# Chunks of 504, 504, 288, 504, 504 tokens in place of 512, 512, 256, 512, 512, and another order of steps around the third chunk

## The chip, the cores and the metric

The kernel runs on one core of a Trainium2 chip. The core has TensorE (PE, matrix products into PSUM), VectorE (DVE), ScalarE (ACT), GpSimd (POOL) and SyncE (SP, which issues most DMAs). The metric is the device time of one execution in microseconds (us), as the median of three runs.

## What is computed

Attention, then two feed-forward blocks, all in float32 on 4 x 576 = 2304 tokens of width 512 (d is 64 wide, 8 heads, scores under a mask of 32 keys: plain for heads 0 to 3, every fourth key for heads 4 to 7):

```python
attn = softmax(where(masks, q @ k.T / 8, -1e9)); x = attn @ v   # 2304 x 512
h = x @ w_in                       # 512 -> 2048
x = (h * (1 / (1 + exp(-h)))) @ w_out   # 2048 -> 512
h = ((x @ w1) * (x @ w2)) @ w3     # 512 -> 1024 -> 1024
out = h @ w_out2                   # 1024 -> 512
```

## The kernel before

Matrices are kept as two parts, a high one (float32 rounded to TensorE's fp32r format) and a low one (what is left), and a product is made of three matmuls: high by high, low by high, high by low.

**Stages.** The instructions of each engine stand in the order in which the program emits them. A list written out by hand (`START`) covers the attention of the first of the four batches, the first chunk of the first feed-forward block and the loading and splitting of `w_in` and `w_out`. Then come the other chunks with the attention of the other batches between them, then the second feed-forward block (lines 840 to 950: products of 384 columns, whose results are combined on VectorE).

**Chunks.** The first feed-forward block takes the tokens in five chunks (`CH1`: start and length). For each chunk it goes through 16 tiles f of 128 hidden units. For a tile, `h_part` makes 12 matmuls `h<-xT,wf` (line 707) with as many columns as the chunk has tokens. `g_tanh` takes half the argument's tanh on ACT (line 721), `g_mul` multiplies on DVE (line 725), `g_high` writes the high part on ACT (line 730) and `g_low` the low part on DVE (line 735). Then `x2_part` makes 12 matmuls `x<-g,wf` (line 747) of the same width into four PSUM banks, which add up over the 16 tiles. Each chunk thus has 16 x 24 = 384 such matmuls. At its end `x2_store` copies the four banks out on ACT and DVE and sends them to DRAM by two DMAs of SP.

**Ring.** The attention writes its output, transposed, into `xT`, which holds only `RING` tokens at a time: token a stands at place a modulo `RING`. `a_high` cuts a piece that goes over the ring's end into two. The fourth and fifth chunk stand where the first and second stood.

**Attention.** It runs in pairs of units (a unit is 192 queries of two heads). `ATT` gives the eight steps of a pair, and `att.step()` emits the next of them: V2S0 (the products with v of an earlier pair and the scores of this one, PE), M (maximum, DVE), E1O3 and E0O2 (exponentials of one unit, three on ACT, line 261, and the write of an earlier unit's output into `xT`, on ACT, line 330, and on DVE, line 323), N (sums and reciprocals on DVE, lines 269 and 271, then the scaling of both units on POOL, line 276), L (loads), T (transposes, PE, line 287) and W (their copy out of PSUM, ACT, line 298).

**Slots.** From the second chunk on, each tile has a slot, a string of letters that are emitted in that order. In the slot of tile f, `h` and `H` are the two halves of the h product of tile f+1, `t` its tanh and multiplication, `g` its high and low part, `x` and `X` the halves of the x product of tile f, `a` one attention step and `m` a piece of weight preparation. The third chunk's slot is the second entry of `SLOT` (index c - 1). Since eight attention steps make a pair and this slot has three, the steps that its three letters `a` stand for change from slot to slot.

```python
T2 = 384
NF = DFF // P      # 16 tiles
ATT = "V2S0|M0|E1O3|E0O2|N0|L1|T0|W0"
hps[c, f] = ps_h.tile([P, 512], F32, tag="h", name=f"h_{c}_{f}")
```

Of the kernel before, what the change touches and what calls it, by code (L numbers as in the profile page):

```python
# [31 lines left out]
KT = DM // P  # L32
NF = DFF // P
NG = DF2 // P
RING = 1280
CH1 = [(0, 512), (512, 512), (1024, 256), (1280, 512), (1792, 512)]
T2 = 384
NPR = NT // (2 * T2)
NSET = NG
# [31 lines left out]
ATT = "V2S0|M0|E1O3|E0O2|N0|L1|T0|W0"  # L71
SLOT = (
    ("ahaHaxtagX", "ahaHxataXg"),
    ("hHataxXag",) * 2,
    ("ahHaaaxtagaXaaa",) * 2,
    ("hmHmxtgmmmmXmmmm",) * 2,
)
# [12 lines left out]
def tile_kernel(  # L90
# [36 lines left out]
    stage = [base.tile([P, 2048], F32, tag=f"wf{NF // 2 + i}", name=f"stage{i}") for i in range(2 * NPAIR)]  # L127
    xT = base.tile([P, KT, 2, RING], F32R, tag="xT", name="xT")
    ident = base.tile([P, P], F32, tag="ident", name="ident")
# [195 lines left out]
    def a_high(n):  # L325
# [7 lines left out]
        def place(a, n_):  # L333

            first = min(n_, RING - a % RING)
            return [(0, first, a % RING)] + ([(first, n_ - first, 0)] if first < n_ else [])

# [7 lines left out]
        while r < DIL:  # L345
            cut = place(b * S + CL * r + mm * u, mm)
            x, n_ = cut[0][2], DIL - r
            while x + (n_ - 1) * CL + mm > RING:
                n_ -= 1
# [345 lines left out]

    NC1 = len(CH1)
    hps, gt, xps = {}, {}, {}
# [4 lines left out]
    def h_kt(c, f, kt):  # L702
        t0, n = CH1[c]
        ps = hps[c, f][:, :n]
        r0 = t0 % RING
        for x, (sa, sb) in enumerate(((0, 0), (1, 0), (0, 1))):
            nc.tensor.matmul(  # L707
                ps, win(f, sa, kt), xT[:, kt, sb, r0:r0 + n],
                start=(kt == 0 and x == 0), stop=(kt == KT - 1 and x == 2),
            )  # L710
# [7 lines left out]
    def g_tanh(c, f):  # L718
        n = CH1[c][1]
        gt[c, f] = gp.tile([P, 512], F32, tag="t", name=f"t_{c}_{f}", bufs=1)[:, :n]  # L720
        nc.scalar.activation(gt[c, f], hps[c, f][:, :n], AF.Tanh, scale=0.5)  # L721

    def g_mul(c, f):
        t, ps = gt[c, f], hps.pop((c, f))[:, :CH1[c][1]]
        nc.vector.scalar_tensor_tensor(t, t, 1.0, ps, op0=ALU.add, op1=ALU.mult)  # L725

    def g_high(c, f):
        n = CH1[c][1]
        g = gp.tile([P, 2, 512], F32R, tag="g", name=f"g_{c}_{f}")[:, :, :n]
        nc.scalar.activation(g[:, 0], gt[c, f], AF.Copy)  # L730
        gt[c, f] = g, gt[c, f]
# [6 lines left out]
    def x2_part(c, f, half):  # L738
        n = CH1[c][1]
        if f == 0 and half == 0:  # L740
            xps[c] = [ps_x.tile([P, 512], F32, tag="x", name=f"x2_{c}_{m}") for m in range(KT)]
        g = gt[c, f] if half == 0 else gt.pop((c, f))
        if half == 0 and type(g) is tuple:
            g = g[0]
        todo = [(m, sa, 0) for m in range(KT) for sa in (0, 1)] + [(m, 0, 1) for m in range(KT)]
        for m, sa, sb in todo[6 * half:6 * half + 6]:
            nc.tensor.matmul(  # L747
                xps[c][m][:, :n], wout(f, sa, m), g[:, sb],
                start=(f == 0 and sa == 0 and sb == 0), stop=(f == NF - 1 and sb == 1),
            )  # L750
# [26 lines left out]
    def b_part(name, hl):  # L777

        i = B_AT[name]
        if i < 2:  # L780
            o = (4 * i + 2 * hl) * RING
            return xflat[:, o:o + 2 * RING].rearrange("p (m t) -> p m t", m=2)[:, :, :T2]
# [402 lines left out]
```

## Time and profile before

| | |
|---|---|
| median of three runs | 809.15 us (809.12 to 811.04) |
| the profiled execution's own time | 809.15 us |
| its span, first to last instruction | 807.4 us |
| PE busy | 795.9 us (99%) |
| DVE busy | 478.2 us (59%) |
| ACT busy | 324.7 us (40%) |
| POOL busy | 55.8 us (7%) |
| mean granted TensorE clock | 0.997 |

The span is what the trace shows; 1.75 us of the time lie around it. The busy time of an engine counts each instruction from its start to its end, and PE's instructions overlap, so gaps between matmuls can hide in it. The spacing of their starts tells more. The granted clock is given as a share of 2.4 GHz.

### The profile page before, as it was taken

What the parts mean: (1) busy time and instruction counts of PE and PEld (TensorE: products, weight loads), DVE (VectorE), ACT (ScalarE), POOL (GpSimd) and SP (SyncE); (2) the same over time, 40 slices, a digit from 0 to 9 for tenths busy, and PEclk for the clock granted to TensorE, in tenths of its full rate; (3) what the DMA queues carried; (4) which work ended last, traced back from release to release, by engine and by line L of the source; (5) the groups of instructions that cost most, each with busy time, mean ns of one, the idle gap of its engine ahead of it and who ended that gap; (6) DMA issues with size and microseconds to landing.
All of it is one profiled execution on the core that took longest, in us unless ns stands there. A gap on an engine that the chain in (4) does not pass through costs nothing.

```text
span 807.4 us, 12941 instructions
## 1 busy us (share of the span) xinstructions
PE 795.9 (99%) x4882; PEld 689.6 (85%) x4882; DVE 478.2 (59%) x1175; ACT 324.7 (40%) x824; POOL 55.8 (7%) x90
## 2 busy tenths in 40 slices
PE   8899999999999999999999999999999999999997
PEld 7788888888889898888888887898889999999996
DVE  6889893533334342222478849588887655774444
ACT  7778773544434542222355536342333111321112
POOL 5010100010101100000000000013200000000000
PEclk9999999999999999999999999999999999999999
DMA  9967650403013002000387426328521660045202
GB/s 251 277 194 234 192 175 16 141 15 90 16 45 111 17 1 79 1 1 0 102 317 273 157 89 215 120 72 312 236 91 41 221 240 22 1 147 205 92 1 78
DMA packets 43454, 98.61 MB, mean 122 GB/s; under 512 B 3968, under 2 KB 21888, under 8 KB 41344
## 3 DMA queue, kind: packets, MB, share of 16 engines
q1 hardware_dynamic: 42784, 96.91, 36.6%
q10 hardware_dynamic: 608, 0.89, 0.4%
q8 instruction: 38, 0.62, 0.3%
q14 instruction: 24, 0.20, 0.1%
HBM read 73.66 MB, written 24.12 MB: 121 GB/s over the span
## 4 chain that ended last, share of the span: by engine, by line
PE 90%; DVE 3%; ACT 2%; DMA 1%; issue 1%; POOL 1%; SPq 0%; POOLq 0%; DVEq 0%; ACTq 0%
PE x L747 24%; PE h L707 24%; PE bank L867 20%; PE o L918 10%; PE wp L686 4%; PE o L231 2%; PE o L311 2%; PE t L287 2%; DMA raw_u<-in_w_out_dram 1%; ACT stage L261 1%; PE s L231 1%; DMA out_dram<-os 0%; ACT sm L261 0%; DVE y L559 0%; DVE wf L602 0%
## 5 line engine op out<-in xcount | busy, mean ns | idle before, releaser
L747 PE MATMUL x<-g,wf 128*128 128x512 f32 (+1 forms) x960 | 215.0, 372 | 2.7 <-ACT g L730 2.7
L707 PE MATMUL h<-xT,wf 128*128 128x512 f32 (+1 forms) x960 | 212.2, 370 | 0.0
L747 PEld LDWEIGHTS x<-g,wf 128*128 128x128 f32 x960 | 168.2, 190 | 33.6 <-ACT g L730 3.1
L707 PEld LDWEIGHTS h<-xT,wf 128*128 128x128 f32 x960 | 167.1, 188 | 30.5
L867 PE MATMUL bank<-xT,wf 128*128 128x384 f32 x864 | 164.5, 336 | 0.4
L867 PEld LDWEIGHTS bank<-xT,wf 128*128 128x128 f32 x864 | 151.4, 188 | 8.7 <-ACT s L885 1.1
L725 DVE SCALAR_TENSOR_TENSOR t<-t,h 128x512 f32<-128x512 f32 (+1 forms) x80 | 50.7, 633 | 123.4 <-ACT t L721 123.4
L918 PE MATMUL o<-wf,wf 128*128 128x512 f32 x432 | 110.7, 393 | 0.0
L721 ACT ACTIVATE t<-h 128x512 f32<-128x512 f32 (+1 forms) x80 | 44.2, 553 | 137.2 <-PE h L707 134.5
L918 PEld LDWEIGHTS o<-wf,wf 128*128 128x128 f32 x432 | 80.1, 188 | 12.8
L735 DVE TENSOR_TENSOR g<-t,g 128x512 fp32r<-128x512 f32 (+1 forms) x80 | 52.7, 659 | 42.6 <-ACT g L730 41.3
L730 ACT ACTIVATE g<-t 128x512 fp32r<-128x512 f32 (+1 forms) x80 | 47.0, 587 | 40.4 <-DVE t L725 40.4
L903 ACT ACTIVATE wf<-c 128x384 fp32r<-128x384 f32 x48 | 25.2, 525 | 86.8 <-DVE c L901 86.5
L885 ACT ACTIVATE s<-bank 128x384 f32<-128x384 f32 x24 | 11.7, 489 | 95.3 <-PE bank L867 84.7
L261 ACT ACTIVATE sm<-sm,nm 128x96 f32<-128x96 f32 x108 | 39.1, 365 | 22.6 <-DVE nm L251 22.6
L686 PE MATMUL wp<-wf,wf 128*128 128x512 f32 x192 | 46.8, 392 | 0.3 <-DVE wf L602 0.3
L276 POOL TENSOR_TENSOR sm<-sm,rs 128x288 f32<-128x288 f32 x36 | 27.5, 777 | 237.5 <-DVE su L269 126.8
L686 PEld LDWEIGHTS wp<-wf,wf 128*128 128x128 f32 x192 | 35.7, 188 | 7.4 <-DVE wf L602 0.7
L892 DVE TENSOR_TENSOR c<-u,bank 128x384 f32<-128x384 f32 x36 | 19.9, 553 | 32.0 <-PE bank L867 31.7
L598 ACT ACTIVATE wf<-y 128x512 fp32r<-128x512 f32 (+1 forms) x40 | 22.7, 584 | 28.5 <-DVE y L559 13.5
L251 DVE CUSTOM_DVE_ANT_0 sm<-o,mask 128x96 f32<-128x96 f32 x102 | 19.7, 254 | 17.5 <-PE o L231 17.3
L867 PE MATMUL bank<-wf,wf 128*128 128x384 f32 x144 | 28.9, 335 | 0.0
(96 smaller groups left out, 767.5 us busy)
## 6 DMA issues: line engine op xcount, KB each, us to landing
rawj<-in_w_dram SPq DMA_DIRECT2D x32, 512.0 KB, 3.7
raw_i<-in_w_in_dram SPq DMA_DIRECT2D x16, 512.0 KB, 4.3
raw_u<-in_w_out_dram SPq DMA_DIRECT2D x16, 512.0 KB, 4.6
setd<-wf SPq DMA_DIRECT2D x8, 1024.0 KB, 3.9
wf<-setd SPq DMA_DIRECT2D x8, 1024.0 KB, 5.2
setd<-wf SPq DMA_DIRECT2D x8, 768.0 KB, 5.9
wf<-setd SPq DMA_DIRECT2D x8, 768.0 KB, 7.3
xb<-x2d SPq DMA_DIRECT2D x12, 384.0 KB, 7.4
```

The costliest lines, as they stand in the source:

```text
L261: nc.scalar.activation(sm[:, j], sm[:, j], AF.Exp, bias=nm[:, j:j + 1], scale=-1.0, accum_out=su[:, j:j + 1],)
L276: nc.gpsimd.tensor_tensor(sm, sm, rs[:, :NB].to_broadcast([P, NB, KB]), op=ALU.mult)
L686: nc.tensor.matmul(wp_ps[i], a[:, i // 2, sa, i % 2 * P:(i % 2 + 1) * P], o[:, sb], start=(jt == 0 and x == 0), stop=(jt == NG - 1 and x = ...
L707: nc.tensor.matmul(ps, win(f, sa, kt), xT[:, kt, sb, r0:r0 + n], start=(kt == 0 and x == 0), stop=(kt == KT - 1 and x == 2),)
L721: nc.scalar.activation(gt[c, f], hps[c, f][:, :n], AF.Tanh, scale=0.5)
L725: nc.vector.scalar_tensor_tensor(t, t, 1.0, ps, op0=ALU.add, op1=ALU.mult)
L730: nc.scalar.activation(g[:, 0], gt[c, f], AF.Copy)
L735: nc.vector.tensor_sub(g[:, 1], t, f32(g[:, 0]))
L747: nc.tensor.matmul(xps[c][m][:, :n], wout(f, sa, m), g[:, sb], start=(f == 0 and sa == 0 and sb == 0), stop=(f == NF - 1 and sb == 1),)
L867: nc.tensor.matmul(b, a_op(s, a, sa, kt), b_op(x, sb, kt), start=(n == 0), stop=(n == 5),)
L903: behind.append((count[0] + 1, lambda: nc.scalar.activation(hi, c[k], AF.Copy)))
L918: nc.tensor.matmul(ops[pr][m], g_block(jj, n, sa)[:, m % 3 * P:(m % 3 + 1) * P], wp_v(f, sb), start=(first_ and x == 0), stop=(last and x ...
```

## The change

```diff
-RING = 1280
-CH1 = [(0, 512), (512, 512), (1024, 256), (1280, 512), (1792, 512)]
+RING = 1296
+CH1 = [(0, 504), (504, 504), (1008, 288), (1296, 504), (1800, 504)]
...
 SLOT = (
     ("ahaHaxtagX", "ahaHxataXg"),
-    ("hHataxXag",) * 2,
+    ("hHatagxXa",) * 2,
     ("ahHaaaxtagaXaaa",) * 2,
```

The number of matmuls stays as it is, and so does their order on PE; those of four chunks have 8 columns fewer, those of the third chunk 32 more. In the third chunk's slots the letter `g` moves from the end to the place behind the second `a`. On ACT this is seen in the slot in which the h product of tile 4 is made. Before, the rows from that tile's tanh (`t_4`) to the next are these (`sm` are a unit's scores, `su` their sums, `o` an attention output, `g` the high part; x3 are three instructions):

```order
L721 ACTIVATE t_4_3193<-h_4_3170 128x256
L261 ACTIVATE sm_3183,su_3196<-sm_3183,nm_3184 128x96 x3
L330 ACTIVATE xT<-o_3141 128x4x48
L261 ACTIVATE sm_3188,su_3214<-sm_3188,nm_3189 128x96 x3
L330 ACTIVATE xT<-o_3148 128x4x48
L730 ACTIVATE g_4_3220<-t_4_3193 128x256
L721 ACTIVATE t_5_3244<-h_5_3223 128x256
```

In the changed kernel the same place on ACT reads:

```order
L721 ACTIVATE t_4_3189<-h_4_3166 128x288
L261 ACTIVATE sm_3179,su_3192<-sm_3179,nm_3180 128x96 x3
L330 ACTIVATE xT<-o_3140 128x4x48
L730 ACTIVATE g_4_3198<-t_4_3189 128x288
L261 ACTIVATE sm_3184,su_3213<-sm_3184,nm_3185 128x96 x3
L330 ACTIVATE xT<-o_3147 128x4x48
L721 ACTIVATE t_5_3240<-h_5_3219 128x288
```

The high part of tile 4 stands ahead of the second unit's exponentials and output, not behind them. The second place is DVE in the slot in which the h product of tile 7 is made. Before, between the multiplication into `t_7` and that into `t_8` (`su` and `rs` are the sums and reciprocals of step N, the last write of `g_7` is its low part):

```order
L725 SCALAR_TENSOR_TENSOR t_7_3365<-t_7_3365,h_7_3346 128x256
L323 TENSOR_TENSOR xT<-o_3302,xT 128x192
L269 TENSOR_SCALAR su_3359<-su_3359 128x3
L271 RECIPROCAL rs_3387<-su_3359 128x3
L269 TENSOR_SCALAR su_3368<-su_3368 128x3
L271 RECIPROCAL rs_3391<-su_3368 128x3
L735 TENSOR_TENSOR g_7_3394<-t_7_3365,g_7_3394 128x256
L725 SCALAR_TENSOR_TENSOR t_8_3414<-t_8_3414,h_8_3397 128x256
```

In the changed kernel the same place on DVE reads:

```order
L725 SCALAR_TENSOR_TENSOR t_7_3361<-t_7_3361,h_7_3342 128x288
L323 TENSOR_TENSOR xT<-o_3298,xT 128x192
L735 TENSOR_TENSOR g_7_3370<-t_7_3361,g_7_3370 128x288
L269 TENSOR_SCALAR su_3355<-su_3355 128x3
L271 RECIPROCAL rs_3386<-su_3355 128x3
L269 TENSOR_SCALAR su_3364<-su_3364 128x3
L271 RECIPROCAL rs_3390<-su_3364 128x3
L725 SCALAR_TENSOR_TENSOR t_8_3410<-t_8_3410,h_8_3393 128x288
```

The low part of tile 7 stands ahead of the sums and reciprocals of step N, not behind them. With the ring of 1296 tokens its end falls on a multiple of 144, and two output pieces that were cut in two (of 32 and 16 elements) are whole (48), so ACT and DVE have two instructions fewer each, in the second chunk.

## Rows read from the trace of the kernel before

**Rows 1.** The page, parts 1: the span and the engines' busy time.
```profile
span 807.4 us, 12941 instructions
...
PE 795.9 (99%) x4882; PEld 689.6 (85%) x4882; DVE 478.2 (59%) x1175; ACT 324.7 (40%) x824; POOL 55.8 (7%) x90
```

**Rows 2.** The chain that ended last: start us, us, what; groups of 256, 512, 384 columns.
```profile
298.58 1.44 PE h L707 x12
311.27 2.72 PE x L747 x12
...
605.86 2.08 PE bank L867 x12
```

**Rows 3.** Waits of PE from 240 to 306 us: us in total, times, longest.
```profile
PE t L287 <- POOL sm L276: 0.7, 1, 0.7
PE x L747 <- ACT g L730: 0.5, 1, 0.5
```

**Rows 4.** Timeline of PE around tile 4 of the third chunk: start us, us, what.
```profile
262.88 1.60 PE L707 MATMUL h<-xT,wf 128*128 128x256 f32 x12
264.95 1.69 PE L747 MATMUL x<-g,wf 128*128 128x256 f32 x12 [0.47 <-ACT g L730]
266.54 1.16 PE L287 MATMUL t<-ident,sm 128*96 128x128 f32 x6
267.46 1.67 PE L707 MATMUL h<-xT,wf 128*128 128x256 f32 x12
```

**Rows 5.** Timeline of PE at two later transposes of the third chunk.
```profile
275.46 1.60 PE L707 MATMUL h<-xT,wf 128*128 128x256 f32 x12
277.74 1.16 PE L287 MATMUL t<-ident,sm 128*96 128x128 f32 x6 [0.68 <-POOL sm L276]
278.65 1.68 PE L747 MATMUL x<-g,wf 128*128 128x256 f32 x12
...
289.54 0.82 PE L287 MATMUL t<-ident,sm 128*96 128x128 f32 x6
290.12 1.67 PE L747 MATMUL x<-g,wf 128*128 128x256 f32 x12
```

**Rows 6.** Timeline of ACT around tile 4: second unit's exponentials, output, high part.
```profile
263.21 0.36 ACT L261 ACTIVATE sm<-sm,nm 128x96 f32<-128x96 f32 x1
...
264.28 0.31 ACT L330 ACTIVATE xT<-o 128x192 fp32r<-128x192 f32 x1
264.49 0.41 ACT L730 ACTIVATE g<-t 128x256 fp32r<-128x256 f32 x1
```

**Rows 7.** Timeline of DVE and POOL around tile 7: sums, scaling, low part.
```profile
276.19 0.16 DVE L269 TENSOR_SCALAR su<-su 128x3 f32<-128x3 f32 x1
...
276.73 1.58 POOL L276 TENSOR_TENSOR sm<-sm,rs 128x288 f32<-128x288 f32 x2 [9.62 <-DVE su L269]
276.75 0.41 DVE L735 TENSOR_TENSOR g<-t,g 128x256 fp32r<-128x256 f32 x1
```

**Rows 8.** Line 276 from 245 to 306 us: ns shortest/median/longest, first and last start.
```profile
L276 POOL TENSOR_TENSOR sm<-sm,rs x8: 663/670/952, 254.4 to 288.8; 128x288 f32<-128x288 f32 x8
```

**Rows 9.** Timeline of PE and ACT in the first chunk.
```profile
27.16 5.74 PE L707 MATMUL h<-xT,wf 128*128 128x512 f32 x24
...
32.74 2.88 PE L747 MATMUL x<-g,wf 128*128 128x512 f32 x12
...
37.23 0.65 ACT L452 ACTIVATE raw_u<-raw_u 128x512 f32<-128x512 f32 x1 [1.13 <-DMA raw_u<-in_w_out_dram]
...
38.98 4.46 PE L747 MATMUL x<-g,wf 128*128 128x512 f32 x12 [2.21 <-ACT g L730]
```

**Rows 10.** Windows: each engine's busy us (count), granted clock, DMA share, GB/s.
```profile
40.00:41.00 1.00, 1.00 (x4) 0.81 (x3) 1.00 (x11) 1.00 (x6) 0.00 (x0) 0.50 0.19 46
43.00:44.00 1.00, 1.00 (x6) 0.79 (x6) 1.00 (x2) 0.79 (x2) 0.95 (x1) 1.00 0.89 332
...
450.00:460.00 10.00, 10.00 (x45) 8.28 (x45) 9.09 (x16) 5.57 (x11) 0.00 (x0) 1.00 0.41 133
```

## The prediction

> **What bounds the kernel now.** I read the page first: PE is busy for 795.9 of 807.4 us [rows 1]. Since busy time can hide gaps, I went on to the chain that ended last. It stays on PE nearly throughout the chunks, and its groups of 12 matmuls show the spacing at which PE really goes: 1.44 us at 256 columns, 2.72 at 512, and 2.08 at 384 in the second block [rows 2], so 120.0, 226.7 and 173.3 ns a matmul. From 256 to 512 the price grows by 106.7 ns for 256 columns, 0.4167 ns each, and a line through these two ends gives 173.3 at 384, which is the third row. So three widths lie on one straight line: 13.3 ns for each matmul and 0.4167 ns for each column.
>
> Then I asked for what PE waits in the third chunk, the only one whose steps move. The view names two waits, 0.5 us for a high part and 0.7 us for the scaling on POOL [rows 3]. It leaves out gaps that overlapping matmuls cover, so I took the differences of starts. At tile 4 [rows 4]: from the h group to the x group 264.95 - 262.88 = 2.07 against 1.44, so 0.63 lost; from that x group to the transposes 1.59 against 1.44, 0.15 lost; from there to the next h group 0.92, where the undisturbed transposes take 290.12 - 289.54 = 0.58 [rows 5], 0.34 lost. At tile 8 [rows 5]: 277.74 - 275.46 = 2.28 against 1.44, 0.84 lost, and 0.91 against 0.58, 0.33 lost. Together 2.29 us. That is all that the reordered steps could give back; the other three pairs of the chunk have nothing of the kind.
>
> One more wait is touched. In the first chunk PE stands still for 2.21 us until a DMA of `w_out` has landed and ACT has worked on it, and the x group behind it then takes 4.46 in place of 2.72 us [rows 9], at a granted clock of 0.50, that is 1.2 GHz, which is back at 1.00 (2.4 GHz) a few us later [rows 10].
>
> **The change part by part.** *Columns.* A chunk has 384 matmuls. Four chunks lose 8 columns in each: 4 x 384 x 8 x 0.4167 ns = 5.12 us. The third gains 32 in each: 384 x 32 x 0.4167 ns = 5.12 us. The number of matmuls stays, so the 13.3 ns a piece do too. The sum is 0, as it must be on a straight line. No row has 504 or 288 columns; the bounds are that 504 costs what 512 costs (no saving, +5.1 us in all) and that the line holds (0). I take the line, since 384 lies on it to the last digit.
>
> *What the saving can't buy.* Ahead of the 2.21 us wait the first chunk has 24 + 12 matmuls [rows 9], which get 36 x 8 x 0.4167 ns = 0.12 us shorter; the wait ends when the DMA does, so 0.12 us are lost there. Elsewhere in the chunks of 504 PE doesn't wait, and I look for an engine that could not follow: the fullest 10 us of the fifth chunk have DVE busy for 9.09 [rows 10]. A slot there (two groups) falls from 5.44 to 5.36 us, which makes 9.09 x 5.44 / 5.36 = 9.23. There is still room, though it is thin; the g instructions of the four chunks get shorter by the same eight elements. I take 0.
>
> *The third chunk at tile 4.* Now ACT does the second unit's exponentials and its output, 264.49 - 263.21 = 1.28 us, and then the high part [rows 6] for which the x group waits. In the new order the high part stands ahead of them, so it comes 1.28 us sooner less 0.19 (the h group that feeds it is 12 x 32 x 0.4167 ns = 0.16 longer, the tanh some 0.03). Being due 0.63 sooner at most, it stops nobody: 0.63 us gained. The exponentials now stand behind 0.41 us of high part, about 0.44 with 288 columns, and 0.19 later through the longer h group; step N waits for them. In return the low part, some 0.4 us on DVE, no longer stands between them and the sums. Estimate: the scaling on POOL, and with it the transposes, come 0.2 us later, at 266.74. PE, with h and x groups of 1.60 us and two of them ahead of 262.88, would be there at 262.88 + 2 x 0.16 + 2 x 1.60 = 266.40. So 0.34 are lost ahead of the transposes, 0.34 in them, 0.68 in place of 1.12: **0.4 us gained**. The bound on the bad side is that the 0.41 us move the transposes in full and the low part gives nothing back: 0.2 gained. On the good side all 1.12.
>
> *The third chunk at tiles 7 and 8.* Here the low part of tile 7 goes ahead of the sums, which waited for nothing else. It takes 0.41 [rows 7], 0.44 with 288 columns, and with 0.19 for the longer h group and tanh the sums start 0.63 later. Against that, the first scaling on POOL runs beside that low part now: POOL's two take 1.58 us, and of the eight in the chunk the longest takes 952 ns where the median is 670 [rows 7, 8]. With the low part out of the way I take 0.28 back. So the transposes come at 277.74 + 0.63 - 0.28 = 278.09, while three groups of PE ahead of them are 3 x 0.16 = 0.48 later by themselves: **0.1 us gained**, within -0.3 (if POOL stays slow) and +1.17 (no wait left).
>
> The Trainium skill ("SBUF — State Buffer", section "Who interferes with whom") says that DVE and GpSimd share a port pair, and that a DVE instruction with two SBUF inputs contends with a GpSimd instruction that reads SBUF; the low part is one. The long scaling agrees; without that rule the 0.28 would not be counted and the sum would be 0.3 higher.
>
> *The rest.* The cut pieces save four short instructions in the second chunk, where PE waits for none of them: 0. Step L's loads, the stores and every DMA of SP and POOL keep their order; the stores carry as many bytes as before.
>
> Sum against the profiled execution's 809.15 us, which is also the median: 0 + 0.12 - 0.4 - 0.1, about -0.4: **808.8 us**.
>
> **The rivals.** *All waits of the third chunk go.* For it: the slots have 0.32 us more each. Against: the chain of exponentials, sums, scaling that ends each wait starts at the same longer h group. It gives 809.15 - 2.29 + 0.12 = 807.0.
>
> *The moved steps only move the waits.* The high part ahead of the exponentials and the low part ahead of the sums delay POOL by more than the longer groups hide. With 0.4 us at each of the two places and the 0.12: 809.15 + 0.92 = 810.1.
>
> *504 is no shorter than 512 for PE* (**slower**). PE may take columns in blocks, or pay for operands of `xT` that start at place 504 or 1008. All h products so far start at multiples of 256 places, so no row excludes it. If 504 costs what 512 does, the time is 809.15 + 5.12 - 0.4 = 813.9. It decides from 1536 matmuls at 1.9 ns each, which is 2.9 us, on. Against it: the straight line through three widths, though all three are multiples of 128.
>
> *The slow stretch of the clock changes.* What the low clock costs in the first chunk is 4.46 - 2.72 = 1.74 us. PE now stands still 0.12 us longer ahead of it; the fall could come at another moment, the stretch be gone or be twice as long: 809.15 - 0.4 - 1.74 = 807.0, or 810.5. The Trainium skill ("TensorE: Matmul & The Clock Gate", section "What's actually happening") says that the gate looks at activity in a window that runs freely and does not start with the kernel. By that rule the stretch could differ between runs of one kernel; the one profile here can't show it.
>
> **How the numbers follow.** Forecast (waits of the third chunk get a little shorter) 0.60, all waits gone 0.12, waits only moved 0.08, the clock's stretch 0.12, half each way, 504 no shorter 0.08. A measurement of this kernel can tell 0.3% (2.4 us) from no change, so faster is below 806.7 and slower above 811.6. None of the cases alone goes below 806.7; the stretch together with vanished waits does, and I give faster 0.07. Slower is the column case, with a little of a longer stretch: 0.09. No change has the remaining 0.84. The forecast's own range is 808.0 to 809.7. The range, 806.9 to 810.5, takes in every case but the column one and vanished waits together with a vanished stretch; each case has some tenths of spread of its own, so I count on it for 8 or 9 in 10.
>
> **What would show it right or wrong.** In the new trace groups of 12 matmuls should take 2.68 us at 504 columns and 1.60 at 288; 2.72 or more at 504 shows the column rival. The x group behind the h group of tile 5 in the third chunk should start without a wait. The two pairs of transposes around tiles 4 and 8 should still wait, 0.3 to 0.8 us each, for POOL. The first scaling of the second of them should be back at about 670 ns. The wait in the first chunk should be 2.3 us, with a granted clock of 0.50 behind it. Wrong would be a wait of PE in the fifth chunk or the stretch up to 600 us that is not in the trace before, or another length of the slow stretch.

## The result, and the profile after

The changed kernel takes 815.73 us (median of four runs, 814.38 to 816.42), the kernel before 809.13 beside it; the ratio is 1.0073 with a 95% interval of 1.0057 to 1.0089. It is slower by 0.7%, outside the range of the prediction, and on the other side.

The profiled execution took 814.38 us, with a span of 812.6. To see where the time went I cut both spans where a chunk's first h group starts. These are the timeline rows of PE at the cuts in the trace before (start us, us, what):

```profile
137.57 2.88 PE L707 MATMUL h<-xT,wf 128*128 128x512 f32 x12
241.51 1.59 PE L707 MATMUL h<-xT,wf 128*128 128x256 f32 x12
304.18 2.91 PE L707 MATMUL h<-xT,wf 128*128 128x512 f32 x12
389.99 2.88 PE L707 MATMUL h<-xT,wf 128*128 128x512 f32 x12
479.75 2.88 PE L747 MATMUL x<-g,wf 128*128 128x512 f32 x12
```

And the same cuts after the change, with the x group behind the first chunk's wait on top:

```profile
39.18 2.99 PE L747 MATMUL x<-g,wf 128*128 128x504 f32 x12 [1.25 <-ACT g L730]
136.16 2.92 PE L707 MATMUL h<-xT,wf 128*128 128x504 f32 x12
240.28 1.76 PE L707 MATMUL h<-xT,wf 128*128 128x288 f32 x12
307.02 2.90 PE L707 MATMUL h<-xT,wf 128*128 128x504 f32 x12
393.26 2.92 PE L707 MATMUL h<-xT,wf 128*128 128x504 f32 x12
483.90 2.88 PE L747 MATMUL x<-g,wf 128*128 128x504 f32 x12
```

The differences of these starts give the stretches. The last column is what the straight line of the prediction gives for the groups in each (0.04 us less for a group of 504, 0.16 more for one of 288). In the first row the three groups ahead of the wait would save 0.12, but the wait ends with the DMA and takes that back.

| stretch | before | after | difference | straight line |
|---|---|---|---|---|
| start to the x group behind the first chunk's wait | 38.98 | 39.18 | +0.20 | 0.0 |
| from there to the second chunk | 98.59 | 96.98 | -1.61 | -1.2 |
| second chunk | 103.94 | 104.12 | +0.18 | -1.2 |
| third chunk | 62.67 | 66.74 | +4.07 | +4.9 |
| fourth chunk | 85.81 | 86.24 | +0.43 | -1.1 |
| fifth chunk, to its last x group | 89.76 | 90.64 | +0.88 | -1.3 |
| from there to the end | 327.62 | 328.69 | +1.07 | 0.0 |

The third chunk pays for its 32 columns, as expected and a little less. The three later rows with chunks of 504 don't pay back: they get longer, where they should get 1.1 to 1.3 us shorter. The first chunk only seems to pay. In the profile before, its x group behind the wait ran at 1.2 GHz and took 4.46 us [rows 9, 10]; here it takes 2.99 at full clock, as this window shows (columns as in [rows 10]), and that alone is 1.5 us. This slow stretch comes and goes between executions of one kernel (below), so that part is luck of the profiled execution:

```profile
40.00:41.00 1.00, 1.00 (x6) 0.84 (x5) 1.00 (x13) 0.85 (x5) 0.00 (x0) 1.00 0.34 65
```

The chain after the change, read as in [rows 2], shows the price of a group of 12 in each chunk, first to fifth:

```profile
42.17 2.71 PE h L707 x12
...
48.29 2.75 PE x L747 x12
...
160.51 2.76 PE h L707 x12
...
296.08 1.58 PE x L747 x12
297.66 1.59 PE h L707 x12
...
360.66 2.72 PE h L707 x12
363.38 2.74 PE x L747 x12
...
409.90 2.76 PE h L707 x12
```

At 504 columns the groups here take 2.71 to 2.76 us; the line gives 2.68, and 512 columns took 2.72 [rows 2]. So a matmul with fewer columns costs as much, or more. At 288 it takes 1.58 or 1.59, a little under the line's 1.60.

The steps around the third chunk went as told. In the timeline of PE the x group behind the h group of tile 5 no longer waits, and the two transposes still do:

```profile
262.96 1.76 PE L707 MATMUL h<-xT,wf 128*128 128x288 f32 x12
264.56 1.74 PE L747 MATMUL x<-g,wf 128*128 128x288 f32 x12
266.46 1.16 PE L287 MATMUL t<-ident,sm 128*96 128x128 f32 x6 [0.17 <-POOL sm L276]
...
276.00 1.76 PE L707 MATMUL h<-xT,wf 128*128 128x288 f32 x12
278.38 1.16 PE L287 MATMUL t<-ident,sm 128*96 128x128 f32 x6 [0.62 <-POOL sm L276]
```

The losses, by differences of starts: from 264.56 to 266.46 it is 1.90 against an undisturbed 1.58, so 0.32 lost, from 276.00 to 278.38 it is 2.38 against 1.59, 0.79 lost; within the transposes 0.34 and 0.33 as before. Together 1.78 against 2.29 before. The timeline of POOL has the second pair's scaling undisturbed, 1.29 us for two against 1.58 [rows 7]:

```profile
277.66 1.29 POOL L276 TENSOR_TENSOR sm<-sm,rs 128x288 f32<-128x288 f32 x2 [10.62 <-DVE su L269]
```

### The profile page after: what moved, and what is told of

Read it like the earlier page. It is cut to its first block, busy times and chain, and to the rows that moved or that the text cites. A ratio compares the mean times of both kernels' runs of the same rounds, so it can differ in the third digit from the quotient of the medians.

```text
span 812.6 us, 12938 instructions
## 1 busy us (share of the span) xinstructions
PE 802.1 (99%) x4882; PEld 695.3 (86%) x4882; DVE 477.4 (59%) x1173; ACT 324.7 (40%) x822; POOL 55.5 (7%) x90
## 4 chain that ended last, share of the span: by engine, by line
PE 91%; DMA 4%; DVE 2%; ACT 1%; POOL 1%; issue 1%; SPq 1%; POOLq 0%; DVEq 0%; ACTq 0%
PE x L747 24%; PE h L707 24%; PE bank L867 21%; PE o L918 11%; PE wp L686 5%; DMA stage<-in_v_dram 2%; PE o L231 2%; PE o L311 2%; PE t L287 1%; DMA raw_u<-in_w_out_dram 1%; ACT sm L261 0%; SPq L191 0%; DMA out_dram<-os 0%; POOL sm L276 0%; DVE y L559 0%
## 5 line engine op out<-in xcount | busy, mean ns | idle before, releaser
L747 PE MATMUL x<-g,wf 128*128 128x504 f32 (+1 forms) x960 | 216.2, 372 | 1.3 <-ACT g L730 1.3
L707 PE MATMUL h<-xT,wf 128*128 128x504 f32 (+1 forms) x960 | 215.3, 373 | 0.0
L707 PEld LDWEIGHTS h<-xT,wf 128*128 128x128 f32 x960 | 169.5, 188 | 30.6
L725 DVE SCALAR_TENSOR_TENSOR t<-t,h 128x504 f32<-128x504 f32 (+1 forms) x80 | 50.5, 631 | 129.1 <-ACT t L721 129.0
L721 ACT ACTIVATE t<-h 128x504 f32<-128x504 f32 (+1 forms) x80 | 44.2, 553 | 142.5 <-PE h L707 141.4
L735 DVE TENSOR_TENSOR g<-t,g 128x504 fp32r<-128x504 f32 (+1 forms) x80 | 52.6, 657 | 42.2 <-ACT g L730 41.0
L730 ACT ACTIVATE g<-t 128x504 fp32r<-128x504 f32 (+1 forms) x80 | 47.0, 587 | 41.7 <-DVE t L725 41.7
```

What stands on the lines that cost most here:

```text
L707: nc.tensor.matmul(ps, win(f, sa, kt), xT[:, kt, sb, r0:r0 + n], start=(kt == 0 and x == 0), stop=(kt == KT - 1 and x == 2),)
L735: nc.vector.tensor_sub(g[:, 1], t, f32(g[:, 0]))
L747: nc.tensor.matmul(xps[c][m][:, :n], wout(f, sa, m), g[:, sb], start=(f == 0 and sa == 0 and sb == 0), stop=(f == NF - 1 and sb == 1),)
```

## The experiments

The moving operand of a matmul is the one whose columns stream through PE (rows of `xT`, or `g`); the weights are the other, a 128 x 128 part of a `wf` tile. A place is one float32 element in a row. Three theories stood at the start. A: PE takes columns in whole blocks, and 504 is 512 to it. B: the price lies in the start of the moving operand, since the h groups that start at place 504 are the dearest (2.76). A third is that the new order of steps is at fault. The runs led to a fourth, D: the price depends on how the moving operand lies to the weights that are loaded beside it, and on the width. The kernel before ran beside each batch, at medians of 809.75 to 809.93 us.

**The two parts of the change, each alone.** `chunks_only` has the new `CH1` and `RING` with the old slot, `slot_only` this one line:

```diff
-    ("hHataxXag",) * 2,
+    ("hHatagxXa",) * 2,
```

> The chunks of 504, 504, 288, 504, 504 with the old order of steps in the third chunk. If the widths are the cause (theories A and B), the time stays near that of the whole change or above it, since the old order has the longer waits: 815.5 to 816.5. If the new order of steps were the cause, it would be near 809.

> The old chunks with the new order of steps in the third chunk. Theories A and B: the order alone gives a small gain by its two places, 0.3 to 0.9 us, so 808.3 to 808.8. If the order of steps were the cause of the loss: 812 or more.

The chunks alone take 816.10 us (ratio 1.0079, 1.0065 to 1.0094), all of the loss. The order alone takes 810.77 (1.0011, 1.0000 to 1.0022): no gain, against the 0.3 to 0.9 us that I expected. Its third chunk, cut as above, takes 62.75 us (243.97 to 306.71) against 62.67, and the timeline of PE shows why:

```profile
265.33 1.60 PE L707 MATMUL h<-xT,wf 128*128 128x256 f32 x12
266.77 1.60 PE L747 MATMUL x<-g,wf 128*128 128x256 f32 x12
268.93 1.16 PE L287 MATMUL t<-ident,sm 128*96 128x128 f32 x6 [0.55 <-POOL sm L276]
...
277.84 1.60 PE L707 MATMUL h<-xT,wf 128*128 128x256 f32 x12
280.27 1.16 PE L287 MATMUL t<-ident,sm 128*96 128x128 f32 x6 [0.83 <-POOL sm L276]
```

The x group starts on time (1.44 behind the h group), and what it gains is lost ahead of the transposes: 2.16 against 1.44, where it was 1.59 before, and 2.43 at the second pair, where it was 2.28. In the whole change the order gives nothing either: the third chunk takes 66.66 us with the chunks alone (240.46 to 307.12) and 66.74 with both. The half microsecond of waits that went comes from the wider chunk: with the chunks alone, the same sums over the two places give 1.70 us lost, against 1.78 with both and 2.29 before.

**The price of a matmul by width.** The computation is left out; there are only groups of 36 matmuls, one line for each case:

```python
for i in range(36): nc.tensor.matmul(banks[i // 12 % 4][:, :504], w(i), mv[:, 0:504],
                                     start=(i % 12 == 0), stop=(i % 12 == 11))
```

> This kernel leaves out the whole computation: it loads two tiles of numbers and makes groups of 36 matmuls of one width each, 12 to an accumulation as in the h products, and writes a copy of one bank to the output, so only its spacing of matmuls counts. First 23 widths from 256 to 512 with operands that start at place 0, then 512, 504, 384 and 288 columns with other starts. Theory A (columns are paid in whole blocks): a group of 36 costs 36 x 226.7 ns = 8.16 us at 504, 508 and 510 as at 512, and the steps of the curve show the block: 496 costs 7.92 with blocks of 16 and 8.16 with blocks of 32 or 64; 480 costs 7.68 with blocks of 32 and 8.16 with blocks of 64. Theory B (the price lies in the start of the moving operand): all widths at start 0 lie on the straight line (504: 8.04, 496: 7.92, 480: 7.68, 288: 4.80), and 512 columns from places 4, 8 or 16 cost more than 8.16. The straight line alone (my prediction): no steps and no dependence on the start.

The chain of this run, groups of 36 with 256, 288, 384, 448, 480, 488, 496, 504 and 512 columns, all from start 0:

```profile
27.20 4.31 PE b L121 x36
...
40.34 4.74 PE b L124 x36
...
72.60 6.24 PE b L130 x36
...
99.14 7.29 PE b L134 x36
...
113.96 7.82 PE b L136 x36
121.78 8.12 PE b L137 x36
129.89 8.04 PE b L138 x36
...
146.09 8.16 PE b L140 x36
...
170.62 8.20 PE b L143 x36
```

For one matmul that is 119.7, 131.7, 173.3, 202.5, 217.2, 225.6, 223.3, 226.7 and 227.8 ns. The straight line gives 120.0, 133.3, 173.3, 200.0, 213.3, 216.7, 220.0, 223.3 and 226.7. So there are no whole blocks: with blocks of 16 or more 488 would cost what 496 costs, and with smaller ones 504 would lie on the line, below 512. But there is no straight line either: 288 lies 1.6 under it, and 448 to 504 lie 2.5 to 8.9 over it. (The 8.9 is that of 488, which did not repeat: 480, 488, 496 and 504 took 7.80, 7.92, 8.04 and 8.16 us in the run `starts` below, so 488 was 3.3 over.) Three widths that are multiples of 128 had hidden that. The first matmuls behind a change of width or start can be dearer; once they are past, 504 and 512 columns both go at 226.7 ns. The 8 columns save nothing.

**Start 8 places later, at the old widths.** xT is moved by 8 places, and its rows get 16 places longer to make room:

```diff
-    xT = base.tile([P, KT, 2, RING], F32R, tag="xT", name="xT")
+    xTf = base.tile([P, KT, 2, XS], F32R, tag="xT", name="xT")    # XS = RING + 16
+    xT = xTf[:, :, :, 8:8 + RING]
```

> The chunks of before, with xT shifted so that each h product's moving operand starts 8 places (32 bytes) behind a multiple of 16 places; the rows of xT get 16 places longer. Theory A (whole blocks of columns): the width is 512 as before, so 809.1, with h groups of 2.72 us. Theory B (starts): each h group gets longer; with 0.04 us for a group, as the h groups of the second and fifth chunk show after the change (2.76), 80 groups give 3.2 us, so about 812; if the start made the whole loss, 815 or more.

It takes 816.32 us (1.0083, 1.0070 to 1.0096), as much as the whole change, with all widths as before. Its h groups take 2.80 us, and its x groups 2.74:

```profile
319.69 2.74 PE x L749 x12
322.43 2.80 PE h L709 x12
```

So a bad place costs more than B's 3.2 us. But this kernel also has longer rows. `wide_ring` has these alone, with the view at `0:RING`:

> The kernel of before with rows of xT of 1296 places in place of 1280, of which 1280 are used; widths and starts within a row are as before. Theory D: the h and x groups of 512 columns cost up to 2.75 us in place of 2.72 and those of 384 in the second block 1.05 in place of 1.04, so 810 to 813. Theory A: nothing changes, 809 to 810. Against the run shifted by 8 places (816.3) it tells the rows' length from the start.

813.36 us (1.0040, 1.0026 to 1.0054): about half of it comes from the rows' length. h groups take 2.77, x groups 2.72:

```profile
321.76 2.77 PE h L709 x12
324.53 2.72 PE x L749 x12
```

**Width alone.** Chunks, starts and rows as before; only the matmuls are cut:

```diff
+            w_ = n - 8 if n == 512 and (kt, x) != (0, 0) else n
             nc.tensor.matmul(
-                ps, win(f, sa, kt), xT[:, kt, sb, r0:r0 + n],
+                ps[:, :w_], win(f, sa, kt), xT[:, kt, sb, r0:r0 + w_],
```

(and likewise in `x2_part`)

> The kernel of before, with its chunks, starts and rows of xT; only the matmuls of the chunks of 512 leave out their last 8 columns (all but the first of each accumulation), so 8 of 512 tokens get wrong sums. Straight line: 4 x (16 x 11 + 188) x 3.33 ns = 4.9 us less, 805. Theory A and D for the width alone: 504 costs what 512 costs, 809 to 810, and groups of 12 take 2.70 to 2.75 us. If all of the loss lay in the starts and the rows' length, groups of 2.68 us.

811.34 us (1.0011, 0.9998 to 1.0023): leaving out 8 of 512 columns of these matmuls buys nothing that shows, where the line gives 4.9 us. The chain:

```profile
318.74 2.72 PE x L749 x12
321.46 2.73 PE h L708 x12
```

**Where both operands start.** Again without the computation:

> Like the run of widths, this kernel leaves out the whole computation and makes groups of 36 matmuls: 512 and 504 columns from ten starts of the moving operand each, then the same with one weights operand for all matmuls and with weights that start 8 places later, then some widths from start 0 once more. Theory D (the price of a matmul depends on where its two operands lie, the start of the moving one and that of the weights that are loaded beside it, and on the width, and 512 from a round start is a cheap case): 512 costs 8.16 us from starts 0, 64, 128, 256 and 512 and 8.23 to 8.40 from 8, 16, 32, 504; with weights 8 places later the cheap starts change; 504 costs 8.16 or more from most starts. Theory A (whole blocks of columns): 504 costs what 512 costs from each start, and nothing depends on the weights' place. Straight line: 504 costs 0.12 us less than 512 from each start.

The chain, in this order: 512 columns from starts 0, 8, 16 and 504; 504 columns from 504; 512 from 0 and 8 with one weights operand for all 36; 512 from 0 and 8 with weights that start 8 places later:

```profile
27.38 8.16 PE b L121 x36
35.54 8.40 PE b L122 x36
43.95 8.25 PE b L123 x36
...
93.22 8.40 PE b L129 x36
...
167.50 8.28 PE b L138 x36
...
192.20 8.17 PE b L141 x36
200.37 8.40 PE b L142 x36
...
225.22 8.39 PE b L145 x36
233.61 8.16 PE b L146 x36
```

The last two rows are the ones that settle it against B: with the weights 8 places on, a moving operand at 0 is the dear one (8.39) and one at 8 the cheap one (8.16). 504 columns from 504 cost 8.28 / 36 = 230.0 ns, and the h groups of the second and fifth chunk 2.76 / 12 = 230.0.

**The weights moved in the kernel before.** The sharper form of D says that h and x must get dearer when only the weights move:

```diff
-        return base.tile([P, 2048], F32R, tag=f"wf{i}", name=f"wf{i}")
+        return base.tile([P, 2056], F32R, tag=f"wf{i}", name=f"wf{i}")[:, 8:]
```

> The kernel of before; only the weights tiles wf start 8 places (32 bytes) later, xT and g stay where they are, and all widths are 512, 512, 256, 512, 512. Theory D in its sharper form (what counts is the start of the moving operand less the start of the weights): the h and x groups of 512 columns cost 2.80 us in place of 2.72, though their moving operands have not moved, while the products of line 686 (wp) and 918 (o), whose operands both lie in wf, stay at the spacing of before; 128 groups x 0.08 = 10 us, so about 820. If the moving operand's own start counted: h and x stay at 2.72, wp and o, whose moving operand is moved, get longer by 6.7 ns each, 624 x 6.7 ns = 4.2 us, so about 814. If neither counts: 809 to 810.

818.96 us (1.0109, 1.0086 to 1.0132). But the edit does more than the expectation says. Each of the 16 weights tiles is now 8 places longer, and the kernel reserves them one after the other, so tile i starts 8 x (i + 1) places later: 8 for tile 0, 128 for tile 15. What is reserved behind them, `xT` and `g`, then starts 128 places later, which `starts` has as a cheap distance. The trace bears this out. Most h and x groups rise to 2.79 to 2.81 us, but the x groups of tiles 7 and 15, 64 and 128 places on, stay at 2.72. In the chain:

```profile
326.50 2.81 PE x L747 x12
329.31 2.79 PE h L707 x12
...
354.39 2.72 PE x L747 x12
...
399.00 2.72 PE x L747 x12
...
499.80 13.76 PE wp L686 x58
```

The differences of the single matmuls' starts, from the sixth to the eleventh of each h group, are 233.3, 233.3, 233.7, 232.7, 233.3, 228.8, 233.7 and 227.3 ns for tiles 0 to 7 of the fourth chunk, and the same within 0.1 for tiles 8 to 15. So the price follows the start of one operand less that of the other, and it repeats after 64 places. Tile 5 lies 48 places off, which is 16 the other way round, and costs what a start of 16 costs in `starts` (228.9 there).

The group of 58 products of line 686 takes 13.76 us, where the chain before has 13.47. It should have stayed only if its two operands had moved alike, as the expectation took them to do. They lie in different tiles, 6 or 7 for the weights and 8 to 11 for the moving operand, so here they are 8 to 40 places apart. The rise is no exception to D. Its first 12 products, 16 apart, go at 228.7 ns. One thing doesn't fit: the x groups of tile 5 go at 233.3 ns where its h groups, at the same distance, go at 228.8. So the distance sorts the costs, but it isn't the whole rule.

**The other tiles' places.** `pad` puts an unused tile of 512 bytes behind xT:

> The kernel of before with an unused tile of 512 bytes behind xT, so that all later tiles lie 512 bytes further on, as after the change, while xT keeps its rows. If the longer second block after the change (328.7 us from the last x group to the end, 327.6 before) comes from the other tiles' places: 328.7 and about 810.5. If it comes from the rows of 1296 places in xT: 327.6 and 809 to 810.

809.60 us (0.9997, 0.9986 to 1.0009), and from the last x group to the end 327.7 us (481.95 to 809.63). The later tiles' places cost nothing; the 1.07 us of the second block come with the longer rows of xT, which `wide_ring` has too (328.7, from 483.62 to 812.29).

**Other chunks.** Last, 512, 480, 320, 512, 480 with a ring of 1312:

> Chunks of 512, 480, 320, 512, 480 with a ring of 1312 and the old order of steps (a small pool of the attention is freed with the attention, to make room). From the curve that the run of widths gave (480: 217.2, 320: 146.4, 512: 226.7 ns): 768 x (217.2 - 226.7) + 384 x (146.4 - 120.0) = +2.8 us, less up to 2 us of waits in the third chunk, so 809.5 to 812. Straight line: 0 for the columns, so 807 to 808.5. Theory A with blocks of 64: 480 costs 512, +10 us, 818 or more.

812.92 us (1.0045, 1.0028 to 1.0063), above the end of what I had from the curve: the rows of 1312 places are dear as well, with 2.75 us for the h groups of the fourth chunk, which are 512 wide from place 0. Each row there lies 32 places further on against the weights than the one ahead of it. Of the 12 matmuls every third, the one from an odd row, takes 234 ns, and the others, a multiple of 64 away, 226 or 227. No run pointed to a version that beats the kernel before.

## Why the prediction was wrong

**The step that failed** is the first of the sum, "I take the line, since 384 lies on it to the last digit". The columns are no zero: 504 costs what 512 does (`narrow`, `widths`), so the four chunks' 5.12 us of saving don't come, while the third chunk pays (4.07 us in the profile). The rival "504 is no shorter than 512 for PE" had this step right, with 813.9 us, and I gave it 0.08. Its first mechanism, whole blocks, is wrong (`widths`). Its second, the operands' start, is right in part: it is the start against that of the weights that is shown to count (`starts`, `wshift8`).

**What the prediction didn't see at all** is that the longer ring moves each of the eight rows of xT. I read the ring only as a change of places and cut pieces. A row of 1280 is ten times 128 places, one of 1296 is ten times 128 and 16, so each next row lies 16 places further on against the weights, and products from xT pay: 2.77 for 2.72 in the h groups at the old widths, and 1.07 us in the second block (`wide_ring`, `pad`). In the changed kernel itself, the h groups that start at place 0 show no such price: 2.71 and 2.72 in the first and fourth chunk, against 2.73 at the same width with the short rows (`narrow`). Those that start at 504 take 2.76. The effects don't add up: `narrow` loses about 6 us against the line, `wide_ring` 3.6 us against the kernel before, and with the starts at 504 the chunks alone lose 6.2. They act on the same matmuls, and no run tells how much of the loss in the chunks of 504 belongs to each.

**The third chunk.** The 0.5 us that I gave it did go (2.29 to 1.78 of waits), and each row that I named came: no wait at tile 5, two waits for POOL, the scaling at its usual length. But the reason was wrong. At the old widths the same order gains nothing (`slot_only`, 62.75 for 62.67), and the wider chunk with the old order is as fast as with the new. In `slot_only` the same sums give 0.07 us gained at the first place and 0.16 lost at the second, so for the order alone the bad bounds that I gave were nearer than the values. (The second, -0.3, was itself mis-sized: 0.63 later against 0.48 makes -0.15.) The rival "the moved steps only move the waits" is what the order does.

**The rest.** The wait of the first chunk ends with the DMA, but its length varies, 1.25 us here, 2.54 with the chunks alone and 2.20 with the order alone, where I had said 2.3. The low clock behind it was gone in the profile after, at 1.00 from 40 to 41 us. It was gone behind the 2.54 us too, and there behind the 2.20 (0.50 from 43 to 44 us). It differs between executions of one kernel: in the first batch those of the kernel before with a mean granted clock of 1.000 took 808.3 to 809.8 us, those at 0.996 to 0.998 took 809.6 to 810.9. So the two profiled executions stand 5.2 us apart where the medians stand 6.6. DVE did not become a bound in the fifth chunk, and the cut pieces cost nothing that shows.

**Open.** Why a matmul pays for the place of its operands isn't settled. The costs repeat after 64 places (`wshift8`). That the weights loaded beside the running matmul are the partner is argued from the distance that counts; no run shows the mechanism. Nor is it shown why a price can differ at the same width and distance: the x groups of tile 5 against its h groups (`wshift8`), and 488 columns, with 8.12 us in one of the runs without the computation and 7.92 in the other. The x groups' 2.74 us in `shift8`, where only xT has moved against the weights, lies in the first five of 12 matmuls behind a dear h group (228 to 236 ns); the other seven go at 226 or 227. Why such a start lasts for some matmuls is open too.

## What to carry to other kernels

Three round widths on a straight line don't give the price of an odd one: time the width itself, at the start and row length that it will have, before a plan takes columns from one place and gives them to another. When a buffer's length changes, look at what its rows' starts become against the other operand, not only at what fits. And a step moved ahead of a wait pays only if nothing behind it is the next to be waited for.

## What the runs showed of the hardware

For fp32r matmuls with 128 x 128 weights loaded for each, 512 columns cost 226.7 ns when moving operand and weights start alike, or 64, 128, 256 or 512 places apart, the first matmuls behind a change left out (`starts`: 8.16 to 8.18 us for 36), and up to 233.3 (8.40 / 36) when they lie 8 places apart. The costs at 72 to 128 places are those at 8 to 64 (`wshift8`). Between 448 and 504 columns the price is 2.5 to 3.9 ns over the line through 256 and 512, but for 488 in one of two runs (8.9); at 288 it is 1.6 under it. That 8 places of a start are worth as much as 16 columns of width on the line (6.7 ns) I had not expected.
